# Two chained MLPs behind a retention layer: combined weight blocks split in place, pairs planned in microseconds, all subtractions on VectorE, a ring of PSUM banks

## The chip, the cores and the metric

The kernel runs on one core of a Trainium2 chip. The metric is the device time of one execution in microseconds (us), lower is better. Its engines are TensorE (PE, with PEld for weight loads), VectorE (DVE), ScalarE (ACT), GpSimd (POOL) and SyncE (SP, which issues all transfers of this kernel).

## The reference

```python
def reference(q, k, v, w_in, w_out, alpha, w_in2, w_out2):   # names shortened
    # q, k, v: (4, 8, 576, 64)
    scores = q @ k.T / 8 * decay          # decay = gamma[h] ** (row - col), lower triangle
    x = (scores @ v)                      # to (2304, 512)
    h = x @ w_in                          # (512, 2048)
    x = (max(h, 0) + alpha * min(h, 0)) @ w_out
    h = x @ w_in2
    return (h * sigmoid(1.702 * h)) @ w_out2     # (2304, 512)
```

The weights arrive as 64-bit floats. Products are made in about single precision: each operand is split into a rounded part and a remainder, and three matmuls (high x high, high x low, low x high) are summed.

## The kernel before

The program is one unrolled list of instructions in an order written by hand. `at(time, fn, *args)` puts a call on a list of events, and `run_to(time)` emits all calls due by then; the unit of time is a step of the loop around. Every engine takes its instructions in that order, and SP issues transfers in that order too, so an instruction that waits holds up what is behind it on its engine.

**Attention** comes first (to about 80 us), with the words of the first MLP's weights beside it.

**First MLP** (L692 to L741): 80 steps (chunk `c` of tokens, block `m` of 128 hidden columns). The chunks have 512 tokens, chunk 4 has 256. In step `i` TensorE does `mm1` of step `i` (12 matmuls) and `mm2` of step `i - 2` (12 matmuls); in between, `activate` (two ScalarE passes, one VectorE pass) and `split` (a ScalarE copy that rounds, and a subtraction for the remainder, by VectorE up to step 21 and by GpSimd after) fill one of three slots of `gsf`. The order of the chunks is 0 and 1 interleaved (32 steps), then 2, 4 and 3 (16 steps each).

**The second MLP's weights are made beside the first MLP.** For each of 16 blocks `w_words` loads 64-bit words into a `raw` buffer (two exist), turns them into single precision with one ScalarE pass (`w_abs`, L113) and four VectorE passes (L117, L120, L127, L134) in a `cv` buffer (two exist). Two blocks make a pair. `combine(j)` forms eight sums of quarters of 256 columns (Strassen's scheme in Winograd's form, seven products in place of eight), and stores five transfers for the first product to DRAM (`rg`). `stage(j, i)` does the rest for seven combined blocks: a rounded copy and a remainder into a staging buffer (tag `xf`, three exist, shared with `x_load`), and its store to `sg`. The pairs' times are in steps:

```python
t, t2 = ((26.2, 29.4), (34.4, 35.9))[j] if j < 2 else (29 + 5.2 * j, 30.6 + 5.2 * j)
```

**Second MLP** (L746 to L794): three rounds of 768 tokens. A round is 112 units of six matmuls with 384 columns: 56 for the first product (eight groups `j` of seven units, `unit1`), 56 for the second (`unit2`, seven blocks `i` of eight). The seven units of a group go to PSUM banks `BANK = "abcabcb"`; a bank is read after a unit and the next unit of that letter adds to what is in it. `after1` and `after2` read the banks, form the sums and apply the activation. `g_split` prepares the operands of `unit2` in a ring of four slots of `gsf`, `g_sum` forms combined activations, `r_load` and `r_split` bring the first product's weights, `s_load` the second's. During the second product of rounds 1 and 2, `x2_load` and `x2_step` load and combine the next round's input.

Of the kernel before, what the change touches and what calls it, by code (L numbers as in the profile page):

```python
# [15 lines left out]
NK = DM // 128  # L16
# [17 lines left out]
GSRC = (0, 4, 1, 3, 0, 2, 3)  # L34


@with_exitstack
def kernel(
# [64 lines left out]
    def w_load(key, src):  # L103
        raws[key] = cvp.tile([128, 2 * DM, 2], I32, tag="raw", name="raw", bufs=2)
        w_piece(key, src, 0)
# [40 lines left out]
    def w_words(t, key, src, ahead, d):  # L146
        at(t - ahead, w_load, key, src)
        at(t - ahead + (1.0 if ahead > 2 else 0), w_piece, key, src, 1)
        for i, fn in enumerate((w_abs, w_clamp, w_top, w_low)):
            at(t + d * i, fn, key)  # L150

    def combine(j):
        m0, m1 = cvs[2, 2 * j], cvs[2, 2 * j + 1]
        t = sums[j] = cvp.tile([128, 2, 4, 256], F32, tag="raw", name="sums", bufs=2)
        q = lambda f, c: f[:, c * 256:c * 256 + 256]
        plus = lambda o, x, y, op: nc.vector.tensor_tensor(out=o, in0=x, in1=y, op=op)  # L156
        plus(t[:, 0, 1], q(m1, 0), q(m1, 1), ALU.add)
        plus(t[:, 1, 1], q(m0, 3), q(m1, 3), ALU.add)
        for g in range(2):
            plus(t[:, g, 0], t[:, g, 1], q(m0, 2 * g), ALU.subtract)  # L160
        plus(t[:, 0, 2], q(m0, 0), q(m1, 0), ALU.subtract)
        plus(t[:, 1, 2], q(m0, 2), q(m0, 3), ALU.subtract)
        plus(t[:, 0, 3], q(m0, 1), t[:, 0, 0], ALU.subtract)
        plus(t[:, 1, 3], q(m1, 2), t[:, 1, 0], ALU.subtract)
        nc.sync.dma_start(out=rg[j][:, 0], in_=q(m0, 0))
        nc.sync.dma_start(out=rg[j][:, 3], in_=q(m0, 1))
        nc.sync.dma_start(out=rg[j][:, 6], in_=q(m1, 1))
        nc.sync.dma_start(out=rg[j][:, 1:3], in_=t[:, 0, 0:2])
        nc.sync.dma_start(out=rg[j][:, 4:6], in_=t[:, 0, 2:4])

    def stage(j, i):
        m0, m1, t = cvs[2, 2 * j], cvs[2, 2 * j + 1], sums[j]
        f = (
            m0[:, 512:768], t[:, 1, 0], t[:, 1, 1], m1[:, 512:768],
            t[:, 1, 2], t[:, 1, 3], m1[:, 768:1024],
        )[i]
# [4 lines left out]
        if i == 6:  # L181
            cvs.pop((2, 2 * j)), cvs.pop((2, 2 * j + 1)), sums.pop(j)
# [191 lines left out]
    def split(i, c, m, eng):  # L374
# [4 lines left out]
        sub(eng, gs[:, 1], g, gs[:, 0])  # L379
# [4 lines left out]
    def part_load(c, n):  # L384
        if n:
            parts[c] = cvp.tile([128, NK, 512], F32, tag="raw", name="part", bufs=2)
# [60 lines left out]
    def x2_load(r, k):  # L447
        for h in range(2):
            t = xr[h] = cvp.tile([128, 2, RN], F32, tag="cv", name="xr", bufs=2)
# [9 lines left out]
    def x2_split(i, k, f):  # L459
        hi, lo = xblk(i, k, 0), xblk(i, k, 1)  # L460
        copy(hi, f)
        sub(nc.vector, lo, f, hi)

    def x2_step(k, i):
        a, b = xr[0], xr[1]
        if i == 0:
            x2_split(0, k, a[:, 0])
        elif i == 1:
            add(a[:, 1], a[:, 1], a[:, 0], ALU.subtract)
            x2_split(2, k, a[:, 1])  # L470
        elif i == 2:
            x2_split(3, k, b[:, 0])
        elif i == 3:
            xr[2] = cvp.tile([128, 512], F32, tag="xf", name="xs", bufs=3)[:, 0:RN]
            add(xr[2], b[:, 1], a[:, 1], ALU.subtract)
            x2_split(1, k, xr[2])
        elif i == 4:
            x2_split(5, k, b[:, 1])
        elif i == 5:
            add(a[:, 0], xr[2], a[:, 0], ALU.subtract)  # L480
            x2_split(4, k, a[:, 0])
        else:
            add(b[:, 0], b[:, 0], xr[2], ALU.subtract)
            x2_split(6, k, b[:, 0])
# [39 lines left out]
    def unit1(j, i):  # L524
        b = BANK[i]
        if i < 3:
# [8 lines left out]
            i < 3,  # L535
# [5 lines left out]
    def after1(j, what):  # L541
        a, b, c = (bank.get(k) for k in "abc")
        if what == "s1":
            tm[j] = cvp.tile([128, 5, RN], F32, tag="raw", name="tm", bufs=2)
# [9 lines left out]
        elif what == "u3":  # L554
            add(u3, b, s1)
            add(u3, u3, s5)
        elif what == "g22":
            gelu(gblk(2, j), u3)
# [4 lines left out]
        elif what == "c21":  # L563
            add(c21, b, s1)
# [7 lines left out]
    def gs2(v):  # L572
        return gsf[:, v % 4 * 768:v % 4 * 768 + 768].rearrange("p (c n) -> p c n", c=2)
# [28 lines left out]
    def after2(r, i, d):  # L602
        a, b, c = (bank.get((k, d)) for k in "abc")
        if i == 0:
            tm["o", d] = cvp.tile([128, 5, RN], F32, tag="raw", name="to", bufs=2)
# [10 lines left out]
        elif i == 4:  # L616
            add(u3, b, s1)
            add(u3, u3, s5)
# [30 lines left out]
    with tc.manual_schedule():  # L649
# [40 lines left out]
        gsf = mp.tile([128, 3072], F32R, name="gsf")  # L690
# [8 lines left out]
        for n, (_, c, m0, _) in enumerate(BLOCKS[N_FIRST:], 1):  # L699
            homes[c] = xp[n % 2]  # L700
            for k in range(NK):
                t = starts[c, m0] - (4 if n == 1 else 6) + (0.9 if n == 1 else 1.3) * k
                at(t - 2, x_load, c, k)
# [3 lines left out]
        for j in range(NM // 2):  # L707
            t, t2 = ((26.2, 29.4), (34.4, 35.9))[j] if j < 2 else (29 + 5.2 * j, 30.6 + 5.2 * j)
            t, t2 = base + t, base + t2
            w_words(t, (2, 2 * j), w2, 1.6, 0.35)  # L710
            w_words(t2, (2, 2 * j + 1), w2, 1.6, 0.35)
            at(t2 + 1.4, combine, j)
            for i in range(7):
                at(t2 + 1.9 + 0.22 * i, stage, j, i)
        for k in range(2):
            at(n1 - 9 + 3.3 * k, x2_load, 0, k)
            for i in range(7):
                at(n1 - 7.6 + 3.1 * k + 0.3 * i, x2_step, k, i)
        for n in range(3):
            at(n1 - 2.5, r_load, n)  # L720
# [6 lines left out]
        for i in range(n_s + LAG):  # L727
# [11 lines left out]
            if not last:  # L739
                split(i, *steps[i][:2], nc.vector if i < 22 else nc.gpsimd)  # L740
# [113 lines left out]
```

## Time and profile before

| what | us |
|---|---|
| median of 3 runs (range) | 931.24 (930.59 to 934.09) |
| the profiled execution | 927.77 |
| its span, first to last instruction | 926.0 |
| PE busy (share) | 855.4 (92%) |
| DVE busy | 640.8 (69%) |
| ACT busy | 461.0 (50%) |
| POOL busy | 71.9 (8%) |
| mean granted TensorE clock | 0.967 of full |

The span is what the views of the profile divide; the execution's own time has 1.77 us around it. Busy shares are means over parts with different limits: a matmul's busy time overlaps its neighbours', so the length of a stretch is read from starts.

### The profile page before, as it was taken

To read this page: it belongs to the slowest core of one execution; us is meant where nothing else is said; L and a number is where in the kernel's file an instruction comes from. 1 tells how busy PE (TensorE), PEld (TensorE's weight loads), DVE (VectorE), ACT (ScalarE), POOL (GpSimd) and SP (SyncE) were. 2 spreads that over 40 slices of the span, in tenths; PEclk is the share of its full clock that TensorE was granted. 3 is DMA by queue.
4 is the path that set the end of the run, shared out by engine and by line. 5 is a ranking of instruction groups with operands and counts; after the bars stand their busy time and mean duration, and the time that the engine had idled before them with its cause. 6 is when DMAs were issued, how large, how long until landed. Compare 5 with 4: busy or idle time off the path is not lost.

```text
span 926.0 us, 13960 instructions
## 1 busy us (share of the span) xinstructions
PE 855.4 (92%) x5132; PEld 764.2 (83%) x5132; DVE 640.8 (69%) x1071; ACT 461.0 (50%) x920; POOL 71.9 (8%) x61
## 2 busy tenths in 40 slices
PE   9899999999999977685599999999899998999998
PEld 8787888888888766574488889998899997999998
DVE  4987867884766766463674457778867778777676
ACT  5544555543444343233434456565456564566553
POOL 0000000012222221111122200000000000000000
PEclk9999999999999988877899999999899999999999
DMA  9884634342564437464442343487443686533872
GB/s 322 304 306 174 233 111 162 137 160 74 190 207 154 152 138 226 151 187 159 158 145 73 97 129 119 156 302 273 148 133 119 236 274 237 162 120 113 313 264 96
DMA packets 58484, 166.96 MB, mean 180 GB/s; under 512 B 6704, under 2 KB 18608, under 8 KB 52656
## 3 DMA queue, kind: packets, MB, share of 16 engines
q1 hardware_dynamic: 58416, 166.08, 53.1%
q8 instruction: 40, 0.66, 0.3%
q14 instruction: 28, 0.23, 0.1%
HBM read 128.83 MB, written 37.22 MB: 179 GB/s over the span
## 4 chain that ended last, share of the span: by engine, by line
PE 62%; DVE 14%; DMA 12%; ACT 6%; issue 4%; SPq 2%; DVEq 0%; ACTq 0%
PE acc L518 21%; PE acc L400 14%; PE h L357 14%; PE h L518 9%; DMA sg<-stage 5%; DMA raw<-in_w_dram 4%; DVE sums L156 2%; PE av L225 2%; DVE ws L86 2%; DMA xr<-x 1%; DVE gsf L86 1%; ACT ws L83 1%; DVE tm L428 1%; DVE g L369 1%; ACT g L539 1%
## 5 line engine op out<-in xcount | busy, mean ns | idle before, releaser
L400 PE MATMUL acc<-gsf,w 128*128 128x512 f32 (+1 forms) x960 | 224.9, 384 | 45.6 <-ACT gsf L83 25.5
L400 PEld LDWEIGHTS acc<-gsf,w 128*128 128x128 f32 x960 | 176.6, 199 | 82.9 <-ACT gsf L83 28.1
L357 PE MATMUL h<-x,w 128*128 128x512 f32 (+1 forms) x960 | 215.0, 375 | 0.0
L357 PEld LDWEIGHTS h<-x,w 128*128 128x128 f32 x960 | 173.0, 196 | 31.0 <-DVE w L86 0.7
L83 ACT ACTIVATE gsf<-g 128x384 fp32r<-128x384 f32 (+2 forms) x248 | 131.0, 541 | 117.1 <-DVE g L369 77.1
L518 PE MATMUL acc<-x,ws 128*128 128x384 f32 x720 | 139.4, 339 | 5.2 <-DVE tm L428 5.2
L518 PE MATMUL acc<-gsf,ws 128*128 128x384 f32 x720 | 134.4, 344 | 8.5 <-DVE gsf L86 7.8
L518 PEld LDWEIGHTS acc<-gsf,ws 128*128 128x128 f32 x720 | 128.4, 193 | 13.5 <-DVE gsf L86 12.4
L518 PEld LDWEIGHTS acc<-x,ws 128*128 128x128 f32 x720 | 124.5, 188 | 12.8 <-DVE tm L428 12.8
L86 DVE TENSOR_TENSOR gsf<-g,gsf 128x384 fp32r<-128x384 f32 (+1 forms) x191 | 105.6, 569 | 35.7 <-ACT gsf L83 34.8
L86 POOL TENSOR_TENSOR gsf<-g,gsf 128x512 fp32r<-128x512 f32 (+1 forms) x57 | 71.7, 1258 | 460.4 <-ACT gsf L83 423.2
L369 DVE SCALAR_TENSOR_TENSOR g<-h,nalpha_sb,g 128x512 f32<-128x512 f32 (+1 forms) x80 | 55.5, 693 | 74.2 <-ACT h L368 74.2
L86 DVE TENSOR_TENSOR ws<-rw,ws 128x512 fp32r<-128x512 f32 x96 | 59.1, 620 | 39.0 <-ACT ws L83 39.0
L367 ACT ACTIVATE g<-h 128x512 f32<-128x512 f32 (+1 forms) x80 | 43.8, 547 | 62.1 <-PE h L357 60.9
L539 ACT ACTIVATE g<-tm 128x384 f32<-128x384 f32 x72 | 37.9, 526 | 43.0 <-DVE tm L428 41.9
L518 PE MATMUL h<-x,ws 128*128 128x384 f32 x288 | 57.8, 335 | 0.0
L428 DVE TENSOR_TENSOR tm<-acc,tm 128x384 f32<-128x384 f32 x96 | 53.0, 552 | 3.8 <-ACT ws L83 2.0
L518 PE MATMUL h<-gsf,ws 128*128 128x384 f32 x288 | 51.5, 335 | 1.0 <-DVE gsf L86 1.0
L428 DVE TENSOR_TENSOR g<-g,g 128x384 f32<-128x384 f32 x93 | 51.5, 554 | 1.1
L83 ACT ACTIVATE ws<-rw 128x512 fp32r<-128x512 f32 x96 | 51.6, 568 | 0.0
L518 PEld LDWEIGHTS h<-gsf,ws 128*128 128x128 f32 x288 | 50.0, 188 | 1.7 <-DVE gsf L86 1.7
L518 PEld LDWEIGHTS h<-x,ws 128*128 128x128 f32 x288 | 50.9, 188 | 0.1
(70 smaller groups left out, 741.9 us busy)
## 6 DMA issues: line engine op xcount, KB each, us to landing
ws<-sg SPq DMA_DIRECT2D x42, 1024.0 KB, 5.1
raw<-in_w_dram SPq DMA_DIRECT2D x64, 512.0 KB, 5.0
sg<-stage SPq DMA_DIRECT2D x56, 256.0 KB, 2.6
ld<-in_qkv_dram SPq DMA_DIRECT2D x15, 864.0 KB, 6.5
rw<-rg SPq DMA_DIRECT2D x24, 512.0 KB, 3.5
rw<-rg SPq DMA_DIRECT2D x24, 384.0 KB, 3.0
kts<-in_kn_dram SPq DMA_DIRECT2D x16, 256.0 KB, 6.6
rg<-sums SPq DMA_DIRECT2D x16, 256.0 KB, 2.0
```

The lines of the kernel that those rows point to most:

```text
L83: return nc.scalar.activation(out=out, in_=in_, func=ACTF.Copy)
L86: return eng.tensor_tensor(out=out, in0=a, in1=b.bitcast(F32), op=ALU.subtract)
L156: plus = lambda o, x, y, op: nc.vector.tensor_tensor(out=o, in0=x, in1=y, op=op)
L225: nc.tensor.matmul(out=out, lhsT=lhsT, rhs=rhs, start=start, stop=stop, skip_group_check=True)
L357: nc.tensor.matmul(out=t, lhsT=w[:, cw, k * 128:k * 128 + 128], rhs=x[:, cx], start=(i == 0), stop=(i == 3 * NK - 1),)
L367: nc.scalar.activation(out=g, in_=t, func=ACTF.Relu)
L369: nc.vector.scalar_tensor_tensor(out=g, in0=t, scalar=nalpha_sb[:, m:m + 1], in1=g, op0=ALU.mult, op1=ALU.add)
L400: nc.tensor.matmul(out=acc[0][d], lhsT=w[:, cw, d * 128:d * 128 + 128], rhs=g[:, cx], start=(m == m0 and i == 0), stop=(m == m1 - 1 and i ...
L428: nc.vector.tensor_tensor(out=out, in0=x, in1=y, op=op)
L518: nc.tensor.matmul(out=out, lhsT=w(cw), rhs=x(cx), start=(start and n == 0), stop=True, skip_group_check=True,)
L539: nc.scalar.activation(out=out, in_=in_, func=ACTF.Gelu_apprx_sigmoid)
```

## The change

- `combine` and `stage` go. `sums1`, `r_store` and `sums2` form and store the sums; `b_hi` writes a block's rounded part over a quarter or sum that is no longer needed, `b_lo` writes the remainder over the block itself, `b_store` stores the two with one transfer each. The sums of a pair live in one of the two `raw` buffers (now named apart as `raw0`, `raw1`) or in two buffers of `xp[0]`.
- `tick(us)` turns microseconds of TensorE time since the first MLP's start into steps; each pair has two start times, two load times, two `raw` slots and a home for the sums.
- `split` subtracts on VectorE in every step.
- `xf` has two buffers in place of three, `gsf` five slots in place of four for the second MLP.
- In the first product letters `a` and `c` take the fixed banks and every `b` unit (1, 4 and 6) starts a new bank of a ring of four; `u3` adds `u2`, and `c21` adds `u3`.
- Times of the second MLP's helpers move: `x2_step` in three phases, `g_split` earlier, `g_sum` spread, `after2`'s two halves 1.1 units apart, `r_split` and `r_load` by up to 2 units (not shown below). Round 1's input is loaded into `xp[0]` buffers in place of `cv` buffers.

```diff
-    def combine(j):
-        m0, m1 = cvs[2, 2 * j], cvs[2, 2 * j + 1]
-        t = sums[j] = cvp.tile([128, 2, 4, 256], F32, tag="raw", name="sums", bufs=2)
...
-    def stage(j, i):
-        m0, m1, t = cvs[2, 2 * j], cvs[2, 2 * j + 1], sums[j]
...
-        o = cvp.tile([128, 2, 256], F32R, tag="xf", name="stage", bufs=3)
-        copy(o[:, 0], f)
-        sub(nc.vector, o[:, 1], f, o[:, 0])
-        nc.sync.dma_start(out=sg[i][j // 4][:, j % 4], in_=o.bitcast(F32))
...
+    def quarter(j, e, c):
+        return cvs[2, 2 * j + e][:, c * 256:c * 256 + 256]
+
+    def sums1(j, home):
+        if home < 2:
+            t = cvp.tile([128, 2, 4, 256], F32, tag=f"raw{home}", name="sums")
+            t = [t[:, g] for g in range(2)]
+        else:
+            t = [xp[0].tile([128, 4, 256], F32, tag=f"x{2 + g}", name="sums") for g in range(2)]
+        sums[j] = t
+        m = [[quarter(j, e, c) for c in range(2)] for e in range(2)]
...
+    def r_store(j):
+        nc.sync.dma_start(out=rg[j][:, 6], in_=quarter(j, 1, 1))
...
+    def block2(j, i):
+        if i in (1, 2, 4, 5):
+            n = {1: 0, 2: 1, 4: 2, 5: 3}[i]
+            return sums[j][0][:, n], sums[j][1][:, n]
+        e, h, l = {0: (0, 3, 2), 3: (1, 0, 2), 6: (1, 1, 3)}[i]
+        return quarter(j, e, h), quarter(j, e, l)
+
+    def b_hi(j, i):
+        hi, f = block2(j, i)
+        copy(hi.bitcast(F32R), f)
+
+    def b_lo(j, i):
+        hi, f = block2(j, i)
+        nc.vector.tensor_tensor(out=f.bitcast(F32R), in0=f, in1=hi, op=ALU.subtract)
+
+    def b_store(j, i):
+        for c, t in enumerate(block2(j, i)):
+            nc.sync.dma_start(out=sg[i][j // 4][:, j % 4, c], in_=t)
+
+    def pair_words(j, t0, t1, l0, l1, slots, home):
+        for e, (t, ld) in enumerate(((t0, l0), (t1, l1))):
+            key = 2, 2 * j + e
+            at(tick(ld), w_load, key, w2, slots[e])
+            at(tick(ld) + 0.01, w_piece, key, w2, 1)
+            for fn, d in ((w_abs, 0.0), (w_clamp, 2.0), (w_top, 3.6), (w_low, 5.2)):
+                at(tick(t + d), fn, key)
+        t = t1 + 7.8
+        at(tick(t), sums1, j, home)
+        at(tick(t + 1.0), r_store, j)
+        at(tick(t + 1.6), sums2, j)
+        t += 2.0
+        for g, blocks in enumerate(((0, 3), (6, 1), (2, 4, 5))):
+            for i in blocks:
+                at(tick(t + 2.8 * g), b_hi, j, i)
+                at(tick(t + 2.8 * g + 2.8), b_lo, j, i)
+                at(tick(t + 2.8 * g + 4.2), b_store, j, i)
...
-        f = cvp.tile([128, 512], F32, tag="xf", name="xf", bufs=3)[:, 0:c1 - c0]
+        f = cvp.tile([128, 512], F32, tag="xf", name="xf", bufs=2)[:, 0:c1 - c0]
...
-        sub(eng, gs[:, 1], g, gs[:, 0])
+        sub(nc.vector, gs[:, 1], g, gs[:, 0])
...
+    def x2_steps(k, t, step, gap):
+        for i in range(7):
+            for phase in range(3):
+                at(t + step * i + gap * phase, x2_step, k, i, phase)
...
-        tag = {"a": "h", "b": f"acc{n}", "c": f"acc{2 + n}"}[what]
-        t = mps.tile([128, 512], F32, tag=tag, name=tag, bufs=4 if what == "a" else 1)
+        tag = {"a": f"acc{n}", "b": "h", "c": f"acc{2 + n}"}[what]
+        t = mps.tile([128, 512], F32, tag=tag, name=tag, bufs=4 if what == "b" else 1)
...
+        new = i < 3 or b == "b"
+        if new:
...
-            add(u3, b, s1)
-            add(u3, u3, s5)
+            add(u3, b, u2)
+        elif what == "c22":
+            add(gblk(2, j), u3, s5)
...
-            add(c21, b, s1)
+            add(c21, b, u3)
...
-        return gsf[:, v % 4 * 768:v % 4 * 768 + 768].rearrange("p (c n) -> p c n", c=2)
+        return gsf[:, v % NG * 768:v % NG * 768 + 768].rearrange("p (c n) -> p c n", c=2)
...
+        elif i == 4.5:
             add(u3, u3, s5)
...
-            t, t2 = ((26.2, 29.4), (34.4, 35.9))[j] if j < 2 else (29 + 5.2 * j, 30.6 + 5.2 * j)
-            t, t2 = base + t, base + t2
-            w_words(t, (2, 2 * j), w2, 1.6, 0.35)
-            w_words(t2, (2, 2 * j + 1), w2, 1.6, 0.35)
-            at(t2 + 1.4, combine, j)
-            for i in range(7):
-                at(t2 + 1.9 + 0.22 * i, stage, j, i)
-        for k in range(2):
-            at(n1 - 9 + 3.3 * k, x2_load, 0, k)
-            for i in range(7):
-                at(n1 - 7.6 + 3.1 * k + 0.3 * i, x2_step, k, i)
+        begins = [0.0]
+        for c, _, _, _ in steps:
+            begins.append(begins[-1] + 6 * NK * (size(c) / 2.4 + 13.3) / 1e3)
+
+        def tick(us):
+            i = max(n for n in range(n_s) if begins[n] <= us)
+            return base + i + (us - begins[i]) / (begins[i + 1] - begins[i])
+
+        for j, plan in enumerate((
+            (143, 158, 133, 150, (0, 0), 0), (188, 198, 180, 189, (0, 1), 2),
+            (214, 222, 196, 206, (0, 1), 2), (238, 246, 222, 230, (0, 1), 0),
+            (262, 276, 253, 267, (1, 0), 1), (291, 304, 282, 297, (0, 1), 0),
+            (320, 334, 312, 327, (1, 0), 2), (349, 357, 328, 342, (1, 0), 2),
+        )):
+            pair_words(j, *plan)
+        x2_steps(0, n1 - 7.2, 0.4, 0.5)
...
-                split(i, *steps[i][:2], nc.vector if i < 22 else nc.gpsimd)
+                split(i, *steps[i][:2])
...
-                    at(z + NU + 1 + 24 * k, x2_load, r + 1, k)
-                    for i in range(7):
-                        at(z + NU + 6.3 + 22 * k + 2.3 * i, x2_step, k, i)
+                    at(z + NU + 1 + 23 * k, x2_load, r + 1, k)
+                    x2_steps(k, z + NU + 5.2 + 23 * k, 2.8, 0.9)
...
-                    at(z + v - 2.8 + 0.5 * lo, g_split, v, lo)
+                    at(z + v - 3.9 + 1.1 * lo, g_split, v, lo)
...
-                at(z + 20.3 + j, g_sum, 0, 4, 0, j)
-                at(z + 34.3 + j, g_sum, 3, 3, 4, j)
+                at(z + 7.3 + 2.4 * j, g_sum, 0, 4, 0, j)
+                at(z + 25.6 + 2.4 * j, g_sum, 3, 3, 4, j)
...
-                    at(z + 8 * i + 8 + 0.05 * d, after2, r, i, d)
+                    at(z + 8 * i + 8 + 1.1 * d, after2, r, i, d)
+                    if i == 4:
+                        at(z + 42 + 1.1 * d, after2, r, 4.5, d)
```

## Rows read from the trace of the kernel before

**Rows 1.** The page: busy tenths and granted clock in 40 slices.
```profile
PE   9899999999999977685599999999899998999998
...
PEclk9999999999999988877899999999899999999999
```

**Rows 2.** Chain of waits, whole span: start us, length us, what.
```profile
80.37 8.60 PE h L357 x36
...
384.54 7.75 DMA sg<-stage
...
533.91 8.16 PE acc L400 x36
```

**Rows 3.** Windows: length, busy us and count by engine, clock, DMA share, GB/s.
```profile
80.00:254.00 174.00, 174.00 (x772) 143.41 (x769) 127.84 (x159) 88.92 (x138) 14.16 (x10) 1.00 0.46 155
254.00:542.00 288.00, 242.45 (x1159) 204.64 (x1158) 167.98 (x256) 114.58 (x239) 57.55 (x47) 0.91 0.46 151
885.00:895.00 10.00, 10.00 (x59) 10.00 (x59) 8.67 (x18) 5.97 (x12) 0.00 (x0) 1.00 0.69 222
```

**Rows 4.** Timeline of TensorE, 399 to 402 us: start, length, instruction.
```profile
399.77 1.60 PE L357 MATMUL h<-x,w 128*128 128x256 f32 x12
401.21 1.00 PE L400 MATMUL acc<-gsf,w 128*128 128x256 f32 x7
```

**Rows 5.** Chain of waits, 540 to 926 us.
```profile
605.73 8.06 DMA xr<-x
...
736.08 8.32 PE h L518 x48
...
802.10 1.04 PE h L518 x6
...
864.20 8.32 PE h L518 x48
...
897.48 24.45 PE acc L518 x141
```

**Rows 6.** Waits, whole span: total us, times, longest us.
```profile
ACT stage L83 <- DMA sg<-stage: 62.3, 27, 7.1
...
PEld acc L518 <- DVE tm L428: 12.8, 24, 1.3
```

**Rows 7.** Timeline, 391 to 394 us; in brackets idle time before and releaser.
```profile
391.75 0.42 ACT L83 ACTIVATE stage<-sums 128x256 fp32r<-128x256 f32 x1 [4.44 <-DMA sg<-stage]
...
393.15 1.39 PE L400 MATMUL acc<-gsf,w 128*128 128x256 f32 x3 [5.13 <-ACT gsf L83]
```

**Rows 8.** DMA issues, 80 to 543 us: count, KB each, median us to landing.
```profile
sg<-stage SPq DMA_DIRECT2D x56, 256.0 KB, 2.6
...
rg<-cv SPq DMA_DIRECT2D x24, 128.0 KB, 1.7
```

**Rows 9.** Timeline, 259.5 to 263 us.
```profile
259.84 2.47 DVE L412 TENSOR_TENSOR part<-acc,part 128x512 f32<-128x512 f32 x4
...
260.55 2.39 SPq L422 DMA_DIRECT2D x<-part  x4
```

**Rows 10.** Groups by form, 80 to 543 us: count, busy us, mean ns, idle before.
```profile
L86 POOL TENSOR_TENSOR gsf<-g,gsf 128x512 fp32r<-128x512 f32 x41 | 57.8, 1409 | 376.6 <-ACT gsf L83 339.3 <-PE acc L400 27.4 <-DVE x L86 9.8
...
L134 DVE SCALAR_TENSOR_TENSOR cv<-raw,cv 128x1024 int32<-128x1024 int32 x30 | 43.2, 1440 | 0.4
...
L127 DVE SCALAR_TENSOR_TENSOR cv<-raw,cv 128x1024 int32<-128x1024 int32 x29 | 39.2, 1351 | 0.3
...
L86 DVE TENSOR_TENSOR gsf<-g,gsf 128x512 fp32r<-128x512 f32 x23 | 15.8, 686 | 9.0 <-ACT gsf L83 9.0
...
L86 POOL TENSOR_TENSOR gsf<-g,gsf 128x256 fp32r<-128x256 f32 x16 | 13.9, 871 | 83.8 <-ACT gsf L83 83.8
```

**Rows 11.** Groups by form of VectorE, 100 to 200 us.
```profile
L134 DVE SCALAR_TENSOR_TENSOR cv<-raw,cv 128x1024 int32<-128x1024 int32 x11 | 13.4, 1215 | 0.0
...
L127 DVE SCALAR_TENSOR_TENSOR cv<-raw,cv 128x1024 int32<-128x1024 int32 x10 | 12.2, 1216 | 0.0
```

More of the change, by code (lines that the diff above doesn't have):

```diff
@@ L34 @@
 GSRC = (0, 4, 1, 3, 0, 2, 3)
+NG = 5
 @with_exitstack
@@ L101, with w_load @@
     both = "p (c n) -> p c n"
-    def w_load(key, src):
-        raws[key] = cvp.tile([128, 2 * DM, 2], I32, tag="raw", name="raw", bufs=2)
+    def w_load(key, src, slot):
+        raws[key] = cvp.tile([128, 2 * DM, 2], I32, tag=f"raw{slot}", name="raw")
         w_piece(key, src, 0)
@@ L146, in w_words @@
     def w_words(t, key, src, ahead, d):
-        at(t - ahead, w_load, key, src)
+        at(t - ahead, w_load, key, src, key[1] % 2)
         at(t - ahead + (1.0 if ahead > 2 else 0), w_piece, key, src, 1)
@@ new lines, in sums2 @@
+    def sums2(j):
+        t = sums[j][1]
+        m = [[quarter(j, e, c) for c in range(4)] for e in range(2)]
+        add(t[:, 1], m[0][3], m[1][3])
+        add(t[:, 0], t[:, 1], m[0][2], ALU.subtract)
+        add(t[:, 2], m[0][2], m[0][3], ALU.subtract)
+        add(t[:, 3], m[1][2], t[:, 0], ALU.subtract)
+    def r_store(j):
+        nc.sync.dma_start(out=rg[j][:, 6], in_=quarter(j, 1, 1))
+        nc.sync.dma_start(out=rg[j][:, 0], in_=quarter(j, 0, 0))
+        nc.sync.dma_start(out=rg[j][:, 3], in_=quarter(j, 0, 1))
+        nc.sync.dma_start(out=rg[j][:, 1:3], in_=sums[j][0][:, 0:2])
+        nc.sync.dma_start(out=rg[j][:, 4:6], in_=sums[j][0][:, 2:4])
@@ L372, in activate, with split @@
         g_t[c, m] = g
-    def split(i, c, m, eng):
+    def split(i, c, m):
         g = g_t[c, m]
@@ L385, in part_load @@
         if n:
-            parts[c] = cvp.tile([128, NK, 512], F32, tag="raw", name="part", bufs=2)
+            parts[c] = cvp.tile([128, NK, 512], F32, tag="raw1", name="part")
         else:
@@ L448, in x2_load @@
         for h in range(2):
-            t = xr[h] = cvp.tile([128, 2, RN], F32, tag="cv", name="xr", bufs=2)
+            if r:
+                t = cvp.tile([128, 2, RN], F32, tag="cv", name="xr", bufs=2)
+            else:
+                t = xp[0].tile([128, 2, RN], F32, tag=f"x{2 * k + h}", name="xr")
+            xr[k, h] = t
             f = t.rearrange("p c n -> p (c n)")
@@ L457, in x2_load, with x2_step @@
                     )
[L459 to L481, printed above, removed]
-        else:
-            add(b[:, 0], b[:, 0], xr[2], ALU.subtract)
-            x2_split(6, k, b[:, 0])
+    def x2_step(k, i, phase):
+        a, b = xr[k, 0], xr[k, 1]
+        if phase == 0:
+            if i == 1:
+                add(a[:, 1], a[:, 1], a[:, 0], ALU.subtract)
+            elif i == 3:
+                xr[k, 2] = cvp.tile([128, 512], F32, tag="xf", name="xs", bufs=2)[:, 0:RN]
+                add(xr[k, 2], b[:, 1], a[:, 1], ALU.subtract)
+            elif i == 5:
+                add(a[:, 0], xr[k, 2], a[:, 0], ALU.subtract)
+            elif i == 6:
+                add(b[:, 0], b[:, 0], xr[k, 2], ALU.subtract)
+            return
+        f = (a[:, 0], a[:, 1], b[:, 0], xr.get((k, 2)), b[:, 1], a[:, 0], b[:, 0])[i]
+        n = (0, 2, 3, 1, 5, 4, 6)[i]
+        hi, lo = xblk(n, k, 0), xblk(n, k, 1)
+        if phase == 1:
+            copy(hi, f)
+        else:
+            sub(nc.vector, lo, f, hi)
+    def x2_steps(k, t, step, gap):
+        for i in range(7):
+            for phase in range(3):
+                at(t + step * i + gap * phase, x2_step, k, i, phase)
     def r_load(n):
@@ L534, in unit1 @@
             ],
-            i < 3,
+            new,
         )
@@ L543, in after1 @@
         if what == "s1":
-            tm[j] = cvp.tile([128, 5, RN], F32, tag="raw", name="tm", bufs=2)
+            tm[j] = cvp.tile([128, 5, RN], F32, tag=f"raw{j % 2}", name="tm")
             copy(tm[j][:, 0], a)
@@ L604, in after2 @@
         if i == 0:
-            tm["o", d] = cvp.tile([128, 5, RN], F32, tag="raw", name="to", bufs=2)
+            tm["o", d] = cvp.tile([128, 5, RN], F32, tag=f"raw{d}", name="to")
         s1, u2, s5, u3, c11 = (tm["o", d][:, n] for n in range(5))
@@ L689 @@
         mps = pool("mps", 1, space=bass.MemoryType.PSUM, reuse_waits="tile")
-        gsf = mp.tile([128, 3072], F32R, name="gsf")
+        gsf = mp.tile([128, 768 * NG], F32R, name="gsf")
         steps, starts = [], {}
@@ L702 @@
                 t = starts[c, m0] - (4 if n == 1 else 6) + (0.9 if n == 1 else 1.3) * k
-                at(t - 2, x_load, c, k)
+                at(t - 1.6, x_load, c, k)
                 at(t, x_split, c, k, xp[n % 2])
@@ L739 @@
             if not last:
-                split(i, *steps[i][:2], nc.vector if i < 22 else nc.gpsimd)
+                split(i, *steps[i][:2])
         run_to(n1 + 10)
```

47 lines of the change are left out of this document (15 added, 32 removed).

## The prediction

> **What bounds the kernel now.** I read the page's busy slices first, then the chain of waits in order of time, then the waits, then single stretches.
>
> TensorE is the engine to follow: its slices show nines up to a third of the span, a dent to 5 and 6, then eights and nines [rows 1]. The chain gives the length of each part. The first MLP runs from 80.37 to 533.91 + 8.16 = 542.07 [rows 2], which is 461.7 us. What its matmuls need by themselves: 36 matmuls of 512 columns take 8.16 us [rows 2], so a dozen 2.72, and at that pace the windows show TensorE busy 174.00 of 174 us up to 254 us [rows 3]; 12 of 256 columns in 401.21 - 399.77 = 1.44 us [rows 4]. A step has two such dozens, and there are 64 wide steps and 16 narrow ones (chunk 4): 64 x 5.44 + 16 x 2.88 = 394.2 us. So 67.5 us are lost, all after 254 us, where the chain leaves TensorE for DMA pieces such as the 7.75 us one of `sg<-stage` [rows 2].
>
> The second MLP runs from 542.07 to 897.48 + 24.45 = 921.93 [rows 2, 5], 379.9 us. A unit is six matmuls of 384 columns, 8.32 us for 48 [rows 5], so 1.04; three rounds of 112 units need 349.4. Lost: 30.4. By stages of 58.2 us: round 2's second product takes 802.10 - 736.08 = 66.0 (7.8 lost), round 3's first 864.20 - 802.10 = 62.1 (3.9 lost), its second 57.7 (nothing lost) [rows 5]. With 4 us for each first product, 12 are lost there; 18.4 remain for the second products of rounds 1 and 2, the two that also prepare the next round's input.
>
> What ends these waits is in the waits view [rows 6]. ScalarE waited 62.3 us in 27 pieces for a staging buffer whose store had not landed. The engine is in order, so the split of the activations stands behind that wait: at 391.75 a staging copy starts after 4.44 us of waiting, the `gsf` copy comes next, and TensorE starts at 393.15 after 5.13 us without work [rows 7]. The other row is 24 waits of the weight loads for VectorE's `tm`, 12.8 us: once in each of the 24 groups of seven units.
>
> **The change, part by part.**
>
> *Staging removed.* The rounded part goes into a block whose value is spent and the remainder over the block itself, so the wait for one of three buffers goes. The number of copies (7 per pair) and subtractions (7) stays; the stores double in number, 56 of 256 KB to 112 of 128 KB. The nearest rows are 2.6 us for the first and 1.7 us for a 128 KB store [rows 8]: 3.4 us in place of 2.6 for a block, on queues and not on TensorE. On SP's queue the extra 56 issues cost at most 2.39 / 4 = 0.6 us each [rows 9], 34 us over the 245 us that the plan uses; loads of weights and `x_load` stand behind them, and the plan asks for those 4 to 10 us ahead. I cost the queue at nothing; without that cover it is the second rival. The Trainium skill speaks against the split: its page "Perfetto Trace Analysis", section "DMA Optimizations", says that transfers under 2 KB carry a large overhead and should be batched, and here runs of 2 KB become runs of 1 KB. By it the stores would cost 56 x 0.8 = 45 us more of DMA time (an estimate from that section and the two landing rows); the kernel would pay only where something waits for a landing.
>
> *Pairs planned in us.* Before, pairs from the third on were 5.2 steps apart: 28 us in wide steps, but 5.2 x 2.88 = 15 us in the narrow ones. Now they are 23 to 40 us of TensorE time apart, from 133 to 377 us of the 394. The plan is also where the new waits hide: `w_abs` of a pair comes 2 us or less after the planned store of the previous pair's first block in the same `cv` buffer (pairs 2, 4, 5, 6), and three `w_load` calls come within 2 us of the release of their buffer. A landing takes 1.7 us [rows 8], so each may hold ScalarE for 1 to 3 us. A wide step covers it: the activations of a step are wanted four dozens of matmuls, 10.9 us, after its first product ends, and three operations of ScalarE and two of VectorE at 0.6 to 0.7 us with their handovers need some 4. A narrow step has 5.8 us, needs 3, and has 2.5 to 3 to spare.
>
> *GpSimd's 57 subtractions on VectorE.* 41 x 0.686 [rows 10] + 16 of half the columns at 0.4 (between 0.34, half of it, and all of it) = 35 us more. GpSimd's own take 1.409 and 0.871 us [rows 10], so those remainders arrive some 0.6 us earlier. What comes back: while GpSimd worked, VectorE's two integer passes averaged 1.440 and 1.351 us, against 1.215 and 1.216 in the stretch where it hardly did [rows 10, 11]: 30 x 0.225 + 29 x 0.135 = 11 us. VectorE was busy 127.8 of 174 us before 254 us with no loss, and 168 us after it [rows 3]. That becomes 168 + 35 - 11 = 192 in the 220 us that TensorE needs there: 87%. Round 3 shows 8.67 of 10 with TensorE at 10.00 [rows 3]. So it is hidden on average, and tight in the narrow steps (an estimate: two operations of 0.45 in a step's 2.88 us, and for a pair two words of four passes, 1.2, 1.2 [rows 11] and two that I set at 0.7, with fifteen operations of 256 columns at 0.4: 13.6 us in each 26, so 84%, and the split of chunk 3 beside it). Bounds: nothing, and 35 us if nothing hides it. The skill has a rule here too: "Perfetto Trace Analysis", section "Optimizing Scalar/DVE Operations", would offload a saturated VectorE to other engines, even GpSimd, though it adds that the two share a port. The first half would make this part cost up to the 35 us above, the second half little; the slower integer passes speak for the second.
>
> For the first MLP I keep 5 us of the 67.5 (between 0, as in the stretch up to 254 us, and 15: five to seven of the waits named, at 2 to 3 us).
>
> *The ring of banks.* In the first product the `b` bank was read (`u3`) and then accumulated into by unit 6 with one unit of 1.04 us between; that is the 24-fold wait. Now units 1, 4 and 6 each start a fresh bank of a ring of four, and the sums carry `u2` and `u3` along. VectorE's count per group stays at seven. All 12 us go; bounds 0 and 12 left, and I take 0, because the reader named in the row has no successor any more. The first bank `a` now waits for the first MLP's last `acc0`, which is copied while matmuls of three other banks run: nothing. Round 1's input is also split later (its second half ends one step after the last first product instead of two before), 11 operations of VectorE at about 0.5 us; the first unit comes 8.16 us, three dozens of `mm2` [rows 2], after that product. Nothing, or 5.5 us if VectorE is behind by that much.
>
> *Second product.* The activation ring goes from 4 to 5 slots, the copy is issued 1.1 units earlier, `g_sum` calls go from every unit to every 2.4, the input's preparation is cut into add, copy and subtraction 0.9 units apart, and `u3`'s two adds are parted. Before, in units 28 to 44, VectorE had about 16 splits + 8 sums + 11 of the preparation + 4 = 39 operations; at 8.67 / 18 = 0.48 us each [rows 3] that is 18.7 us in 16.6. After, 40 in units 25.6 to 44.4: 19.2 in 19.6. The fresh input still comes late (a transfer of 8.06 us [rows 5], load and copy as far apart as before), but the fifth slot gives about one unit more. So of 18.4 us I keep 4, 2 per round; bounds 0 and 18.4.
>
> *Sum.* 926.0 - 67.5 - 30.4 = 828.1 us with every loss gone; + 5 + 0 + 4 = 837.1. Around the span the profiled execution has 927.77 - 926.0 = 1.8: 838.9. It lies 3.5 us under the median of the runs (931.24): **842 us**.
>
> **Rivals.**
>
> *1. The second product keeps its loss.* VectorE at 98% there leaves no slack, and the first late transfer is unchanged. For: a full VectorE was the state in which those units lost time. Against: round 3's second product, with no input to prepare, loses nothing. 842 + 14 = 856.
>
> *2. Waits for stores come back in another place:* `w_abs` and `w_load` behind landings, SP's head blocked by a store that waits for a subtraction. For: eight pairs reuse two `cv` and two `raw` buffers, with margins of 2 us. Against: the margins in wide steps. Eight pairs x 3 us: 842 + 24 = 866. The skill's rule on small transfers would work in this direction.
>
> *3. VectorE becomes the bound in the first MLP.* 35 us unhidden less the 5 taken: 842 + 30 = 872. Against: 87%.
>
> *4. Slower: every in-place write waits for a whole buffer.* If a copy into one quarter waited for the store of another quarter of the same buffer, each of the 56 blocks would stand a landing and an issue, 1.7 + 0.4, in ScalarE's queue: 118 us on 832.9 (all losses gone), 951. It decides from 98 / 56 = 1.75 us unhidden for each block. Against: four adds into slices of one `part` buffer ran back to back in 2.47 us while four stores of its slices were issued between them [rows 9]; so slices are waited for one by one.
>
> **How the numbers follow.** Forecast 842 (its own range 832 to 852): 0.66. Rival 1: 0.12. Rival 2: 0.12. Rival 3: 0.06. Rival 4 and mixtures of 2 and 3 that eat the whole gain: 0.04. The range has 833 (every loss gone, on the scale of the median) at its foot, one us under it for spread, and goes to 862, past rival 1 and near rival 2: 832 to 862, with 15 in 100 above and 4 below. Half a per cent is 4.7 us, about what this measurement tells from none. Faster 0.96, same 0.01, slower 0.03.
>
> **What would show it.** No `stage` tile; no waits of ScalarE for `sg`; TensorE's clock at full in the slices where it fell, since in the slices from 0.35 to 0.5 it fell where TensorE was idle [rows 1]; the first MLP's length near 399 us; a stage of the first product at 58 to 59 us, without the 24 waits; the second products of rounds 1 and 2 at 60; VectorE near 87% busy and GpSimd empty after the attention. Wrong would be: weight loads waiting for `gsf` by VectorE in chunk 4 (rival 3), ScalarE's `cv` waiting for stores (rival 2), or stores serialised with the in-place copies (rival 4).

## The result and the profile after

The changed kernel takes 854.91 us (median; 851.27 to 855.84) beside 930.91 us for the kernel before on the same chip: a ratio of 0.917, 95% interval 0.914 to 0.921. That is 76 us; 89 were forecast. 854.9 lies inside the stated range of 832 to 862, but above the forecast's own 832 to 852. The profiled execution has a span of 853.3 us, where the forecast's sum had 837.1.

The page of the changed kernel, busy time by engine and the slices that answer to [rows 1]:

```profile
PE 830.4 (97%) x5132; PEld 755.2 (88%) x5132; DVE 633.2 (74%) x1128; ACT 457.9 (54%) x920; POOL 0.2 (0%) x4
...
PE   8999999999999999899998989999999999999998
...
PEclk8999999999999999899999999999999999999999
```

The dent is nearly gone, and the granted clock dips only at the start and in slice 17. VectorE's busy time fell from 640.8 to 633.2 us although it took over 57 subtractions. The chain of waits, in answer to [rows 2] and [rows 5]:

```profile
82.90 8.60 PE h L394 x36
...
353.37 2.90 PE acc L437 x12
...
498.59 1.62 PE acc L558 x6
...
558.64 8.32 PE acc L558 x48
...
791.60 8.32 PE acc L558 x48
...
841.52 7.81 PE h L558 x45
```

The first unit of the second MLP starts at 498.59, the last ends at 841.52 + 7.81 = 849.33. Against the forecast's span:

| part | forecast, us | measured, us |
|---|---|---|
| to the first MLP's start | 80.4 | 82.9 |
| first MLP | 394.2 + 5 = 399.2 | 415.7 |
| second MLP | 349.4 + 4 = 353.4 | 350.7 |
| rest | 4.1 | 4.0 |

The first row is no part of the change: in the profiles of this study, with the attention's code the same, that start lay between 79.5 and 83.9. The second MLP lost 1.3 us where 4 were kept. The first MLP lost 21.5 where 5 were kept: 9.9 in chunk 4's narrow steps, 7.4 in chunk 3, 3.6 in the handover to the second MLP (11.7 us from the end of its last first product in place of 8.2), the rest before chunk 4 (lengths from TensorE's timeline less the matmuls' own time).

Windows of the changed kernel (columns as in [rows 3]): chunk 2, chunk 4, chunk 3.

```profile
254.00:339.00 85.00, 85.00 (x377) 70.38 (x376) 57.27 (x97) 37.67 (x72) 0.00 (x0) 1.00 0.53 178
339.00:398.00 59.00, 53.85 (x388) 50.98 (x387) 40.09 (x82) 28.03 (x71) 0.00 (x0) 0.94 0.61 198
398.00:487.00 89.00, 84.51 (x373) 68.73 (x372) 59.84 (x111) 41.34 (x84) 0.00 (x0) 0.98 0.49 165
```

VectorE is busy 40.09 of 59 us in chunk 4 (68%), so on average it is not full there. What happens at the change from chunk 2 to chunk 4 is in the timeline (start, length, engine, in brackets the wait):

```profile
340.36 0.81 SPq L110 DMA_DIRECT2D raw<-in_w_dram  x2
...
341.22 0.42 SPq L178 DMA_DIRECT2D rg<-cv  x1
...
346.99 0.42 ACT L84 ACTIVATE cv<-cv 128x256 fp32r<-128x256 f32 x1 [1.84 <-DMA rg<-cv]
...
348.34 0.42 ACT L84 ACTIVATE sums<-sums 128x256 fp32r<-128x256 f32 x1 [0.93 <-DMA rg<-sums]
...
350.15 1.10 ACT L114 ACTIVATE cv<-raw 128x1024 f32<-128x1024 f32 x1
...
352.03 1.07 ACT L84 ACTIVATE o<-acc 128x512 f32<-128x512 f32 x2
...
352.54 1.28 DVE L458 COPY o<-acc 128x512 f32<-128x512 f32 x2
...
353.37 2.90 PE L437 MATMUL acc<-gsf,w 128*128 128x256 f32 x12 [3.44 <-DVE o L458]
```

Words for the next pair are issued just ahead of the stores for the first product (`rg`: quarters of the blocks, from `cv`, and sums). ScalarE's in-place copies wait for those stores, a word's first pass of 1.1 us follows, and the accumulators of chunk 2, finished at about 348.3, are copied only from 352.0 on. VectorE's copies stand behind work that needs ScalarE. TensorE waits 3.44 us, and behind that wait its granted clock is 0.50 of full from 353.4 to 358.6 us, the lower of its two levels (1.2 of 2.4 GHz); a dozen narrow matmuls takes 2.56 us there in place of 1.44.

That wait is the longest of the first MLP and not the only one. Two more, of 1.73 and 2.67 us, come where VectorE has no gap: word passes and sums stand ahead of the copy and of the remainder that TensorE needs. TensorE's timeline, and windows of 8.1 and 5.3 us around the waits (columns as above):

```profile
410.67 3.01 PE L437 MATMUL acc<-gsf,w 128*128 128x512 f32 x12 [1.73 <-DVE o L458]
...
458.46 4.09 PE L437 MATMUL acc<-gsf,w 128*128 128x512 f32 x10 [2.67 <-DVE gsf L87]
```

```profile
402.90:411.00 8.10, 6.37 (x35) 5.21 (x34) 8.00 (x15) 2.87 (x7) 0.00 (x0) 1.00 0.23 83
454.20:459.50 5.30, 2.63 (x10) 1.74 (x10) 5.26 (x10) 3.06 (x5) 0.00 (x0) 0.89 0.51 176
```

VectorE is busy 8.00 of 8.10 and 5.26 of 5.30 us there, so a share of 68% over a chunk hides stretches in which it is full.

### The profile page after: what moved, and what is told of

The parts are those of the page before. It is cut to its first block, busy times and chain, and to the rows that moved or that the text cites. A ratio compares the mean times of both kernels' runs of the same rounds, so it can differ in the third digit from the quotient of the medians.

```text
span 853.3 us, 14011 instructions
## 1 busy us (share of the span) xinstructions
PE 830.4 (97%) x5132; PEld 755.2 (88%) x5132; DVE 633.2 (74%) x1128; ACT 457.9 (54%) x920; POOL 0.2 (0%) x4
## 4 chain that ended last, share of the span: by engine, by line
PE 77%; DVE 9%; DMA 6%; ACT 4%; issue 3%; SPq 1%; DVEq 0%; ACTq 0%
PE acc L558 24%; PE h L558 18%; PE h L394 15%; PE acc L437 15%; PE av L262 3%; DMA raw<-in_w_dram 2%; DMA sg<-cv 2%; DVE sums L465 1%; PE st L262 1%; PE sc L262 1%; DMA rg<-sums 1%; DVE g L406 1%; DVE cv L118 1%; ACT cv L114 1%; DVE cv L128 1%
## 5 line engine op out<-in xcount | busy, mean ns | idle before, releaser
L87 DVE TENSOR_TENSOR gsf<-g,gsf 128x384 fp32r<-128x384 f32 (+2 forms) x248 | 141.5, 580 | 51.2 <-ACT gsf L84 49.7
L558 PE MATMUL acc<-x,ws 128*128 128x384 f32 x576 | 112.2, 336 | 2.6 <-DVE o L458 2.6
L558 PE MATMUL acc<-gsf,ws 128*128 128x384 f32 x576 | 101.3, 334 | 0.0
L558 PEld LDWEIGHTS acc<-gsf,ws 128*128 128x128 f32 x576 | 100.0, 188 | 0.0
L558 PE MATMUL h<-x,ws 128*128 128x384 f32 x432 | 87.4, 337 | 0.0
L558 PEld LDWEIGHTS h<-x,ws 128*128 128x128 f32 x432 | 76.8, 190 | 0.0
L558 PEld LDWEIGHTS h<-gsf,ws 128*128 128x128 f32 x432 | 75.0, 188 | 0.0
L404 ACT ACTIVATE g<-h 128x512 f32<-128x512 f32 (+1 forms) x80 | 43.7, 547 | 49.9 <-PE h L394 49.8
L465 DVE TENSOR_TENSOR tm<-h,tm 128x384 f32<-128x384 f32 x72 | 40.0, 555 | 35.8 <-PE h L558 31.5
L84 ACT ACTIVATE ws<-rw 128x512 fp32r<-128x512 f32 x96 | 49.8, 569 | 0.0
L114 ACT ACTIVATE cv<-raw 128x1024 f32<-128x1024 f32 x32 | 36.1, 1128 | 17.5 <-DMA raw<-in_w_dram 13.9
L405 ACT ACTIVATE h<-h 128x512 f32<-128x512 f32 (+1 forms) x80 | 44.0, 550 | 0.0
```

Of the source, the lines that this page charges most:

```text
L84: return nc.scalar.activation(out=out, in_=in_, func=ACTF.Copy)
L87: return eng.tensor_tensor(out=out, in0=a, in1=b.bitcast(F32), op=ALU.subtract)
L114: nc.scalar.activation(out=cvs[key], in_=raws[key][:, :, 1].bitcast(F32), func=ACTF.Abs)
L404: nc.scalar.activation(out=g, in_=t, func=ACTF.Relu)
L405: nc.scalar.activation(out=t, in_=t, func=ACTF.Relu, scale=-1.0)
L465: nc.vector.tensor_tensor(out=out, in0=x, in1=y, op=op)
```

## Experiments

Each ratio is to the kernel before, run beside it on the same chip. Each edit is to the changed kernel, where nothing else is said.

**The banks of the first product, undone** (b in one accumulating bank per group).

```diff
-        tag = {"a": f"acc{n}", "b": "h", "c": f"acc{2 + n}"}[what]
+        tag = {"a": "h", "b": f"acc{n}", "c": f"acc{2 + n}"}[what]
-        new = i < 3 or b == "b"
+        new = i < 3
```

> The changed kernel with the banks of the first product as before (b in one bank per group, units 4 and 6 add to it). If the 24 waits for VectorE's tm are what the ring of banks removed, they return at 0.53 us each, 12.8 us, less up to 2.6 us that the first unit now waits for the first MLP's accumulator: 855 + 10 to 13 = 865 to 868. Rival: VectorE's load was the limit of a group, and the wait only its last sign; then the groups stay near 7.3 us and the time near 855.

852.49 us, ratio 0.917 (0.913 to 0.920): no different from the changed kernel, and none of the 24 waits in its trace. The price of 10 to 13 us fails; the rival's time fits, but its reason (a full VectorE) is not what the next two runs show. What made the waits is hinted at by the kernel before, in the timeline around one of them:

```profile
679.25 0.69 DVE L86 TENSOR_TENSOR ws<-rw,ws 128x512 fp32r<-128x512 f32 x1 [1.91 <-ACT ws L83]
679.86 0.55 DVE L428 TENSOR_TENSOR tm<-acc,tm 128x384 f32<-128x384 f32 x1
...
680.46 1.34 PE L518 MATMUL acc<-x,ws 128*128 128x384 f32 x6 [0.21 <-DVE tm L428]
```

The add `u3` that TensorE needs stood on VectorE behind the remainder of a weight split, which waited 1.91 us for ScalarE's rounded part. The change also moved these splits: remainder 1.2 to 1.9 units behind its rounded part, and past `u3`. Over the whole span VectorE waited 39.0 us for ScalarE in these remainders (96 of them) before the change, and 0.0 after it.

**Old times of those splits, with the new and with the old banks.**

```diff
-                hl, t1 = (((-2.0, -0.7), (-1.5, 0.4)), 1.2) if n % 2 else (((-5.0, -3.8), (-4.5, -3.1)), -2.3)
+                hl, t1 = (((-3.0, -2.5), (-2.0, -1.5)), -0.9) if n % 2 else (((-6.5, -6.0), (-5.5, -5.0)), -4.4)
```

(`r_load` of the next round and the input's second half 0.8 units earlier with them.)

> The changed kernel with the splits of the first product's weights at their earlier times, ring of banks kept. The run with the old banks showed no 24 waits, so either the new times of these splits removed them alone (the remainder no longer stands ahead of u3 on VectorE), or both edits do it, each alone. With the ring kept unit 6 has no wait for u3 in either case: 853 to 858.

> Old times of these splits and old banks together. If the remainder ahead of u3 in VectorE's order made the 24 waits, they are back: 12.8 us on the 852.5 of the run with the old banks alone, 862 to 867. If something else of the change removed them (spread sums, the ring of five slots), 851 to 856.

New banks, old times: 853.44 us (0.918, 0.914 to 0.921). Old banks, old times: 862.51 us (0.927, 0.924 to 0.930), second MLP 362.9 us, and the waits view has them again:

```profile
PEld acc L558 <- DVE tm L465: 11.9, 21, 1.3
```

21 of the 24 waits return, and the second MLP is some 11 us longer than with the old banks alone. So either edit alone removes the wait, and each is worth nothing once the other is there.

**The second product's ring and times, undone.**

```diff
-NG = 5
+NG = 4
-                    at(z + v - 3.9 + 1.1 * lo, g_split, v, lo)
+                    at(z + v - 2.8 + 0.5 * lo, g_split, v, lo)
-                at(z + 7.3 + 2.4 * j, g_sum, 0, 4, 0, j)
-                at(z + 25.6 + 2.4 * j, g_sum, 3, 3, 4, j)
+                at(z + 20.3 + j, g_sum, 0, 4, 0, j)
+                at(z + 34.3 + j, g_sum, 3, 3, 4, j)
-                    x2_steps(k, z + NU + 5.2 + 23 * k, 2.8, 0.9)
+                    x2_steps(k, z + NU + 6.3 + 22 * k, 2.3, 0.0)
```

(the load of the input's second half and `after2`'s times too)

> The changed kernel with the second product as before: four slots for the split activations, splits and sums at their earlier times, add, copy and subtraction of the next round's input in one go. If ring and times removed the 18.4 us that the second products of rounds 1 and 2 lost, the time is 855 + 15 to 19 = 870 to 874. Rival: that loss came with the late transfer of the next round's input alone and depends on other traffic; then it is within 5 us of 855.

868.67 us (0.935, 0.931 to 0.939), second MLP 369.8 us: some 18 us longer than with the change, as expected (ring and times together; their shares were not separated), and the total 14 longer, since this profile's first MLP was 1 us shorter and its start 3 us earlier. The waits for VectorE's remainders are back:

```profile
PEld acc L558 <- DVE gsf L87: 9.8, 8, 2.9
PEld h L558 <- DVE gsf L87: 4.0, 7, 1.4
```

**Pairs in steps again, blocks still split in place.**

```diff
-            pair_words(j, *plan)
+            t, t2 = ((26.2, 29.4), (34.4, 35.9))[j] if j < 2 else (29 + 5.2 * j, 30.6 + 5.2 * j)
...
+                at(t2 + 1.9 + 0.22 * n, b_hi, j, i)
+                at(t2 + 1.9 + 0.22 * n, b_lo, j, i)
+                at(t2 + 1.9 + 0.22 * n, b_store, j, i)
```

(the words' passes, 0.35 steps apart, and the `raw` slots by pair go with them)

> The changed kernel, blocks still split in place, but with the pairs at the times in steps that they had before. If the staging buffers alone held ScalarE, the time stays within 8 us of 855. If the crowding of the pairs in the narrow steps is part of it, ScalarE now waits for the stores of the first product's blocks instead, and half or more of the 46 us that the first MLP gained is lost: 875 to 905.

876.95 us (0.942, 0.938 to 0.947). The first MLP takes 444.0 us, 28 of the 46 it gained are lost. ScalarE now waits in a word's first pass, for its load and for the block's stores that still hold its buffer:

```profile
ACT cv L114 <- DMA raw<-in_w_dram: 32.8, 6, 9.9
...
ACT cv L114 <- DMA sg<-cv: 17.5, 5, 3.7
```

**The kernel before with GpSimd's subtractions on VectorE alone.**

```diff
-                split(i, *steps[i][:2], nc.vector if i < 22 else nc.gpsimd)
+                split(i, *steps[i][:2], nc.vector)
```

> The kernel before with its 57 GpSimd subtractions on VectorE and nothing else changed. If GpSimd slows VectorE's passes and the first MLP is held by the staging stores, the move is worth 0 to 10 us less: 921 to 931. Rival: VectorE lacks the 35 us; 940 to 960.

921.94 us, 0.991 (0.989 to 0.993) of the kernel before: 9 us gained, by that line alone.

**GpSimd's subtractions back in the changed kernel.**

```diff
-        sub(nc.vector, gs[:, 1], g, gs[:, 0])
+        sub(nc.vector if i < 22 or i >= 79 else nc.gpsimd, gs[:, 1], g, gs[:, 0])
```

> The changed kernel with the remainders of steps 22 to 78 on GpSimd again. If VectorE, with these 35 us more, is what costs the first MLP its remaining 21 us, the time falls to 840 to 850. If ScalarE's waits for the stores of the first product's blocks cost them, VectorE's relief gains nothing and the slower integer passes and later remainders cost 0 to 10 us: 855 to 865.

860.74 us (0.926, 0.922 to 0.929), 6 us slower; the first MLP is 422.8 us. Groups by form from 254 to 500 us, this kernel:

```profile
L135 DVE SCALAR_TENSOR_TENSOR cv<-raw,cv 128x1024 int32<-128x1024 int32 x14 | 22.4, 1598 | 0.3
...
L128 DVE SCALAR_TENSOR_TENSOR cv<-raw,cv 128x1024 int32<-128x1024 int32 x14 | 19.9, 1421 | 0.1
...
L121 DVE TENSOR_SCALAR cv<-cv 128x1024 int32<-128x1024 int32 x14 | 14.0, 1000 | 0.5
```

and the changed kernel (254 to 490 us):

```profile
L135 DVE SCALAR_TENSOR_TENSOR cv<-raw,cv 128x1024 int32<-128x1024 int32 x14 | 17.1, 1220 | 0.2
L128 DVE SCALAR_TENSOR_TENSOR cv<-raw,cv 128x1024 int32<-128x1024 int32 x14 | 17.1, 1218 | 0.1
...
L121 DVE TENSOR_SCALAR cv<-cv 128x1024 int32<-128x1024 int32 x14 | 9.7, 694 | 0.5
```

**Five word loads later.**

```diff
-            (214, 222, 196, 206, (0, 1), 2), (262, 276, 253, 267, (1, 0), 1), (291, 304, 282, 297, (0, 1), 0),
-            (320, 334, 312, 327, (1, 0), 2), (349, 357, 328, 342, (1, 0), 2),
+            (214, 222, 196, 209, (0, 1), 2), (262, 276, 256, 267, (1, 0), 1), (291, 304, 286, 297, (0, 1), 0),
+            (320, 334, 315, 327, (1, 0), 2), (349, 357, 328, 345, (1, 0), 2),
```

> The changed kernel with five of the sixteen word loads issued 3 to 4 us later, behind the stores of the sums instead of just ahead of them. If those loads make the stores land late (5.4 us instead of 2) and ScalarE's in-place copies wait for that, the 15 us of such waits shrink to 5 or less and the time falls by 3 to 8 us, to 847 to 852. Rival: VectorE is full there and the stall stays; 854 to 857.

857.9 us (0.922, 0.921 to 0.924): no gain, and the first MLP is 420.3 us, 4.5 longer. That loads ahead of the stores make them land late was right: the DMA issues (count, KB, median us to landing) show it, the changed kernel first, then this one.

```profile
rg<-cv SPq DMA_DIRECT2D x24, 128.0 KB, 5.6
```

```profile
rg<-cv SPq DMA_DIRECT2D x24, 128.0 KB, 1.8
```

But the wait moved. With the in-place copies earlier, a word's first pass comes to the front of ScalarE's queue sooner, and it waits for the blocks' stores, which themselves land later now (`sg<-cv` 3.8 us in the median, 3.0 in the changed kernel); the waits view and the timeline of this kernel:

```profile
ACT cv L114 <- DMA sg<-cv: 13.0, 4, 4.0
```

```profile
421.37 1.12 ACT L114 ACTIVATE cv<-raw 128x1024 f32<-128x1024 f32 x1 [3.97 <-DMA sg<-cv]
422.38 0.62 ACT L84 ACTIVATE gsf<-g 128x512 fp32r<-128x512 f32 x1
...
423.06 3.28 PE L437 MATMUL acc<-gsf,w 128*128 128x512 f32 x12 [3.29 <-ACT gsf L84]
```

In the changed kernel that wait was 1.7 us in all.

**The handover.** The first unit's bank is taken from accumulators that ScalarE empties, and three of the four weight splits for it come later.

```diff
-        tag = {"a": f"acc{n}", "b": "h", "c": f"acc{2 + n}"}[what]
+        tag = {"a": f"acc{1 - n}", "b": "h", "c": f"acc{3 - n}"}[what]
-                    at(n1 + 0.1 + n + 0.45 * q + 0.2 * lo, r_split, n, q, lo)
+                    at(n1 + (0.1 if n + q == 0 else 1.05) + n + 0.45 * q + 0.2 * lo, r_split, n, q, lo)
```

> The changed kernel with the first unit's bank taken from the accumulators that ScalarE empties first (a in acc1 and acc0, c in acc3 and acc2) and three of four weight splits for it placed behind the copies of the first MLP's last accumulators. If the first unit waits for that copy, 2 to 3 us go: 852 to 853. Rival: it waits for the split weights as well; 854 to 856.

850.85 us (0.914, 0.912 to 0.916), below what was expected; the intervals of this run and of the changed kernel overlap, and the first MLP in the traces is 2.0 us shorter (413.8). TensorE's timeline in the changed kernel, and in this one:

```profile
498.59 1.62 PE L558 MATMUL acc<-x,ws 128*128 128x384 f32 x6 [2.62 <-DVE o L458]
```

```profile
496.56 1.32 PE L558 MATMUL acc<-x,ws 128*128 128x384 f32 x6 [0.33 <-ACT o L84]
```

**Both.** The two edits above together.

> Both edits together: their gains add, 845 to 850. If the chain in the first MLP goes on elsewhere, 852 to 856.

856.78 us (0.921, 0.919 to 0.923): the handover does not save it. The first MLP is 419.2 us, 5.4 longer than with the handover alone, as the later loads by themselves cost 4.5.

**Less VectorE work** (the clamp of the second MLP's words is left out).

```diff
+        if key[0] == 1:
             nc.vector.tensor_scalar(
                 out=f, in0=f, scalar1=F64_MIN, scalar2=F64_MAX, op0=ALU.max, op1=ALU.min
```

> The changed kernel without the clamp of the second MLP's words (one VectorE pass of 0.69 us for each of 16 words left out: 11 us less of VectorE, values outside the single range would not be clamped). If a full VectorE costs the 21 us, the first MLP gets shorter by 5 to 11 us: 844 to 850. If ScalarE's waits do, it stays within 3 us: 852 to 856.

847.41 us (0.910, 0.907 to 0.913), first MLP 409.0 us, 7 less. So VectorE's work has a share in the 21 us, as the two full stretches above suggest. TensorE's waits for its accumulator copies fall from 5.2 us to the row below (254 to 500 us), while ScalarE's waits for the `rg` stores stay (8.6 and 6.9 us; 8.2 and 7.0 in the changed kernel):

```profile
PE acc L438 <- DVE o L459: 2.0, 2, 1.4
```

How the 7 us divide among the stalls was not separated.

**Loads and first passes later, with the handover.**

```diff
+            (216, 222, 196, 209, (0, 1), 2), (266, 276, 256, 267, (1, 0), 1), (295, 304, 286, 297, (0, 1), 0),
+            (324, 334, 315, 327, (1, 0), 2), (352, 357, 332, 345, (1, 0), 2),
```

(the handover's lines as above; one more load, of the last pair, comes 4 us later)

> The changed kernel with the handover edit, the five loads later, and the first ScalarE pass of the pairs 2, 4, 5, 6 and 7 two to four us later, so that it no longer comes right behind the stores of the previous pair's first block. If the waits of in-order ScalarE for landings (of the sums' stores before the in-place copies, of the blocks' stores before the next words) cost most of the first MLP's 21 us, the first MLP falls from 414 to 402 to 408 and the time to 838 to 845. If a full VectorE costs them, it stays at 849 to 853.

842.49 us (0.905, 0.902 to 0.908): faster than both kernels. The first MLP takes 404.3 us, 14.9 less than with both edits before; from its first narrow first product to chunk 3's first it takes 49.8 us where the matmuls in between need 48.6, and 58.5 in the changed kernel. Some of its waits from 254 to 500 us:

```profile
ACT cv L114 <- DMA sg<-cv: 6.7, 3, 3.0
...
PE acc L437 <- DVE o L458: 3.3, 1, 3.3
ACT cv L84 <- DMA rg<-cv: 3.3, 2, 2.3
...
ACT sums L84 <- DMA rg<-sums: 2.3, 2, 1.4
```

In the changed kernel the last two were 8.2 and 7.0, and TensorE's wait for `o` was 5.2 in two. ScalarE's waits in a word's first pass for the word's own load were larger than all of these, 9.0 us in the changed kernel and 11.8 here; since they grew while the time fell, the gain did not come from them.

## Why the prediction was right, and where not

*The bound and the floor.* Right in kind: ScalarE's waits for `sg` stores and the crowded pairs held the first MLP, and no run went below the floor of 98 us less (the fastest is 89 us less). By the runs, of the first MLP's 46 us 28 belong to the plan in us; of the other 18, 7 came in the kernel before with the line for GpSimd alone (454.4 against 461.6), and the rest is left to the splitting in place with the other edits of that part. The staged version with pairs planned in us was not run, so what the staging buffers cost by themselves stays open. That the time fell inside the range is in part luck: the range was drawn past rival 1's 856, and rival 1 did not happen.

*"I keep 5 us of the 67.5" is the step that was mis-sized.* It was 21.5 with the handover. The waits that the part on the plan named do exist, but not in the size or at the place that I weighted. I set a landing at 1.7 us from [rows 8]; for the stores for the first product it is 5.6, because the plan issues a word's load when its buffer comes free, and that is just ahead of them. The list of first passes close behind a store was short as well: by the plan's times pairs 3 and 7 have margins of 2 and 1 us too. I priced the waits one by one against the slack of a step; in chunk 4's first step they came ahead of the accumulators' copies, for which a narrow step leaves only 1.4 us, one dozen of matmuls. Rival 2 has most of the mechanism: later loads alone moved the wait, later first passes with them took 9.5 us off the first MLP beyond the handover edit (413.8 to 404.3). Rival 3 has a part: VectorE is full just ahead of two of the waits, and less work on it gave 7 us. These two shares may overlap and were not added up.

*GpSimd.* Right in sign: hidden, and the slower integer passes are real; without them the part even gains. The sum was mis-sized: 168 + 35 - 11 = 192 us for VectorE and 87% counted two passes as slowed. From 254 us to the end of the first MLP it was busy 167.9 us in the kernel before, 167.8 with that line alone changed and 167.0 in the changed kernel: nothing was added on balance, since other passes are shorter too without GpSimd's subtractions, the `int32` `TENSOR_SCALAR` 0.694 in place of 1.000 us for one. Rival 3 in its full size fails, as GpSimd's return costs 6 us. The Trainium skill's advice to offload a saturated VectorE (page "Perfetto Trace Analysis", section "Optimizing Scalar/DVE Operations") was not put to the test, since VectorE was busy only 168 of 288 us there before; its caution that VectorE and GpSimd share a port and that moving work between them might not help agrees with the trace, 1.220 us becoming 1.598.

*Small stores.* The blocks' halved stores landed in 2.0 us (`sg<-sums`) and 3.0 us (`sg<-cv`) where 1.7 were set, but in first passes ScalarE waited only 1.7 us in all for them. The late ones are the stores for the first product, whose size did not change, and the 128 KB ones landed in 1.8 us once the loads were issued later.

*The ring of banks.* "All 12 us go" is right in amount; the reason given, that the reader has no successor any more, is not the only one. The splits' new times removed the wait as well, and I had left them out of the part. The ring cost something instead: the first bank `a`, which now waits for the first MLP's `acc0`, was put at nothing and waited 2.6 us.

*Second product.* Right: 18 us by the run that undid it. I kept 4 by counting VectorE at 98%, 19.2 us in 19.6. The count was right and nothing was lost, as the window of the changed kernel for those units in round 1 shows (VectorE 19.02 us, TensorE and its weight loads without a gap):

```profile
585.00:604.60 19.60, 19.60 (x115) 19.60 (x115) 19.02 (x41) 13.89 (x30) 0.00 (x0) 1.00 0.76 275
```

So a VectorE near its limit was no stall here, where each operation was issued early enough; that was rival 1's premise.

*Scale.* The forecast's span was 16.2 us short (837.1 against 853.3). The 3.5 us added between the profiled execution and the median did not recur (855.1 and 854.9), and by luck they hid a fifth of that error.

## What to carry to other kernels

When a buffer wait on an in-order engine goes, ask which landing the next instruction of that engine will wait for, and what is ahead of that transfer in its queue: a large load issued as soon as its buffer is free makes the small stores behind it late. Look at what stands ahead of the accumulators' copies in the step in which they change hands, on every engine that copies, above all where steps are short. A wait that a view lists by the tile it waits for can be the fault of what stands ahead of that tile's writer: look one instruction back on its engine before redesigning the resource.

## What was unexpected of the hardware

A store of 128 KB took 5.6 us (median of 24) to land behind loads of words issued just ahead of it on the same queue, and 1.8 us when these came later. VectorE's integer passes took 1.220 us without GpSimd and 1.598 beside its subtractions, in the same stretch of two kernels that differ in that line.
